# Another order of all operations, and other buffer homes, in a transformer block's forward and backward pass

## The chip, the cores and the metric

One core of a Trainium2 chip runs the whole program in one launch. The metric is the device time of that core in microseconds, the median of the runs of a kernel. TensorE is called PE below, VectorE DVE, ScalarE ACT, GpSimd POOL and SyncE SP.

## The reference

The kernel computes the output of one pre-LN transformer block and all gradients with respect to its inputs, for S = 2048 rows, D = 512, F = 1792, 32 heads of 16, in bf16:

```python
def _A_ref(x, wqkv, wo):                      # attention in a dilated sliding window
    W, dil = 8, 2
    q, k, v = ...                             # (x @ wqkv), 32 heads of 16
    idx = pos[:, None] - (jnp.arange(W) * dil)[None, :]     # rows s, s-2, ..., s-14
    kg, vg = k[:, :, idx], v[:, :, idx]       # gathered: 8 keys and values per row
    attn = softmax(where(idx >= 0, einsum("bhsd,bhswd->bhsw", q, kg) * scale, -1e9))
    o = einsum("bhsw,bhswd->bhsd", attn, vg)
    return o @ wo
def _B_ref(x, w1, b1, w2, b2):
    return gelu(x @ w1 + b1) @ w2 + b2
h  = x + _A_ref(layernorm(x), wqkv, wo)
h2 = h + _B_ref(layernorm(h), w1, b1, w2, b2)
out, vjp = jax.vjp(f, x, wqkv, wo, w1, b1, w2, b2)
return (out, *vjp(grad_out))
```

## The kernel before

The rows are cut into four chunks of 512. For each chunk there are three stages.

- **First stage**: LN1, the q, k, v projections (L616, L270), the dots of queries with eight keys (one DVE product of 128x4096 per two window places, L468, summed by PE with a matrix of ones, L476), softmax, then the weighted values. For these POOL gathers eight shifted copies of v from DRAM (Ro, 2304 KB, L460), DVE multiplies (prbo, L507), PE sums (L516), ACT evicts (ost, L521). Then wo, the residual and LN2, whose output SP transposes on its way (ln2T, L291).
- **Second stage**: the FFN with gelu (weights w, output xb and gl), its output, and its backward pass to the gradient at the attention's output.
- **Third stage**: the attention's gradient. got is the gradient through wo (ACT evicts it from PSUM, L297), prb the products for the gradient of the attention weights (L468). Then the gradients of q, k and v, each from its own gather on POOL (Rq from k_d, Rk from q_d, Rv from go_d), four DVE products per gather (prbq, prbk, prbv, L507), four sums on PE (L516), and four evictions on ACT (gqs, gks, gvs, L521). At the end the gradient through wqkv and the LN1 backward pass (gyr, u, gx, L550 to L559).

The weight gradients need all chunks and so run beside the third stage. Each is a group of 16 matmuls (L270, or L268 where it is issued as four matmuls of 32 columns between two sums) into one PSUM bank, which ACT evicts (L297) into half of a pair buffer: wgs for the FFN (wgs2 and wgs1 where the two are told apart), wgso and wgsq for the attention. A full pair is stored by SP (L287). The last groups read LN1's output back from DRAM (ln1b, L282).

Nothing is scheduled at run time. `Plan.op` records every operation with its engine and the buffers that it reads and writes; `Plan.emit` then emits them in one given order (ORDER) and gives each buffer a given place (HOMES): an SBUF offset in units of 64 bytes or a PSUM bank. So ORDER sets the order of the instructions of every engine, and of the transfers that SP and POOL issue, each in order. HOMES decides which later buffer overwrites which earlier one, and that is a wait as well: an operation that writes into a new buffer must wait until the last reader of the old one at that place is done. The reader may be a store that is still on its way.

```python
        for b, h in zip(self.bufs, homes):
            b.home = h if b.space == "ps" else self.base + h * 64
```

A weight-gradient group ends like this; the pair's store is an operation of its own in ORDER:

```python
        evict(st, lambda: st()[:, n, :], ps, lambda: ps()[:, 0:N], N, key=n, tag="wge" + tag)
        if n:
            PAIR.clear()
            store(None, lambda: dst.rearrange("(a p) d -> p a d", p=P), st, lambda: st(), N / 2, tag="wgst" + tag)
```

Of the kernel before, what the change touches and what calls it, by code (L numbers as in the profile page):

```python
# [159 lines left out]
def kernel(  # L160
# [1026 lines left out]
    10, 12, 0, 14, 69, 1, 16, 17, 11, 21, 13, 23, 9, 8, 50, 29, 30, 51, 52, 27, 53, 54, 26, 46, 31, 55, 19, 249, 28, 42, 47, 2, 354, 3, 48, 49, 43,  # L1187
    37, 4, 174, 5, 355, 60, 44, 61, 56, 57, 45, 62, 172, 59, 67, 6, 63, 7, 173, 64, 66, 18, 65, 171, 80, 175, 68, 176, 276, 81, 82, 177, 274, 181,
    179, 83, 70, 275, 178, 71, 87, 180, 277, 72, 73, 278, 379, 279, 88, 74, 183, 75, 377, 77, 24, 22, 85, 25, 380, 84, 86, 76, 378, 252, 89, 78, 251,
    381, 98, 280, 110, 382, 20, 282, 105, 96, 97, 79, 99, 92, 283, 102, 90, 114, 93, 100, 91, 94, 101, 195, 184, 284, 108, 188, 95, 281, 32, 194, 286,  # L1190
    189, 196, 112, 192, 190, 126, 109, 185, 149, 217, 285, 111, 39, 113, 115, 186, 383, 116, 385, 117, 191, 187, 215, 118, 193, 201, 208, 292, 352,
    211, 291, 146, 289, 119, 293, 120, 213, 288, 386, 384, 202, 387, 297, 121, 389, 203, 122, 128, 298, 182, 58, 287, 127, 299, 598, 305, 353, 132,
    290, 204, 294, 212, 214, 216, 218, 250, 295, 597, 137, 148, 304, 296, 133, 306, 311, 197, 219, 134, 300, 307, 129, 301, 147, 198, 302, 138, 303,
    140, 220, 394, 38, 199, 221, 130, 139, 391, 316, 392, 131, 200, 209, 314, 135, 395, 136, 205, 141, 401, 308, 400, 142, 332, 318, 388, 396, 143,
    393, 315, 150, 402, 320, 317, 144, 319, 152, 151, 156, 153, 154, 159, 480, 321, 158, 322, 155, 157, 161, 398, 323, 324, 325, 160, 162, 163, 326,
    327, 164, 333, 334, 343, 338, 403, 222, 408, 168, 407, 167, 166, 404, 165, 40, 397, 405, 170, 409, 344, 596, 481, 345, 595, 346, 339, 411, 210,
    410, 335, 347, 503, 348, 399, 509, 340, 41, 223, 229, 349, 523, 224, 390, 336, 230, 513, 337, 510, 417, 351, 341, 514, 517, 145, 599, 350, 527,
    518, 423, 505, 528, 504, 535, 507, 536, 421, 524, 519, 342, 515, 506, 419, 533, 508, 520, 418, 534, 360, 516, 231, 529, 243, 358, 511, 525, 356,
    240, 530, 244, 420, 526, 483, 422, 537, 424, 362, 361, 521, 206, 425, 241, 539, 232, 242, 426, 484, 245, 540, 551, 235, 485, 427, 246, 552, 247,
    233, 414, 363, 236, 406, 234, 366, 543, 237, 482, 357, 248, 259, 364, 238, 207, 531, 367, 257, 359, 544, 365, 239, 541, 368, 260, 369, 602, 264,  # L1200
    253, 370, 258, 373, 255, 263, 372, 545, 256, 371, 254, 374, 428, 261, 547, 559, 376, 262, 553, 265, 169, 266, 548, 601, 546, 435, 549, 267, 542,
    270, 429, 271, 608, 560, 568, 610, 561, 849, 563, 562, 861, 15, 554, 855, 564, 269, 841, 550, 856, 859, 569, 842, 565, 268, 839, 490, 566, 862,
    273, 847, 567, 840, 865, 848, 611, 850, 837, 555, 430, 330, 538, 851, 436, 556, 845, 512, 852, 437, 455, 860, 835, 415, 866, 446, 867, 846, 838,
    857, 586, 557, 604, 570, 868, 686, 449, 571, 447, 702, 696, 687, 609, 703, 416, 680, 438, 697, 458, 450, 836, 457, 690, 858, 558, 577, 522, 674,
    605, 532, 441, 439, 619, 448, 681, 676, 451, 575, 442, 440, 572, 606, 677, 412, 573, 675, 672, 691, 574, 700, 443, 456, 587, 600, 454, 607, 765,
    444, 329, 452, 578, 445, 612, 617, 576, 488, 328, 684, 673, 620, 701, 682, 579, 603, 487, 461, 453, 590, 591, 272, 670, 225, 489, 683, 459, 580,
    694, 462, 588, 486, 615, 685, 592, 584, 695, 613, 413, 581, 671, 628, 764, 589, 618, 762, 465, 614, 726, 460, 463, 582, 622, 688, 583, 692, 585,
    633, 693, 593, 624, 616, 431, 678, 623, 626, 594, 631, 466, 679, 625, 706, 930, 753, 627, 707, 927, 629, 891, 763, 714, 468, 106, 659, 464, 469,
    125, 704, 643, 124, 744, 727, 644, 632, 718, 754, 892, 853, 660, 634, 755, 636, 730, 107, 918, 637, 745, 929, 698, 375, 652, 715, 766, 470, 331,
    719, 735, 748, 467, 708, 635, 746, 630, 756, 645, 928, 728, 699, 653, 494, 736, 729, 34, 654, 471, 731, 689, 472, 747, 733, 737, 710, 473, 732,  # L1210
    661, 638, 475, 757, 895, 720, 662, 709, 734, 869, 773, 433, 751, 843, 711, 774, 716, 749, 639, 844, 712, 893, 493, 705, 312, 717, 863, 871, 713,
    875, 721, 309, 750, 795, 655, 752, 646, 777, 477, 723, 796, 872, 476, 760, 791, 739, 722, 474, 758, 313, 784, 432, 738, 740, 479, 780, 778, 879,
    896, 900, 725, 880, 621, 742, 883, 724, 741, 876, 919, 909, 743, 884, 759, 798, 931, 761, 792, 885, 901, 785, 870, 922, 873, 864, 886, 1016, 923,
    103, 874, 881, 781, 35, 789, 1036, 790, 920, 877, 902, 1004, 1037, 910, 1017, 1020, 911, 1010, 1021, 878, 894, 800, 904, 799, 1008, 913, 1006,
    1009, 914, 434, 782, 1011, 897, 663, 1030, 1005, 882, 786, 783, 887, 1031, 801, 889, 921, 1034, 898, 888, 1007, 1014, 787, 491, 656, 310, 899,
    1024, 854, 958, 104, 1025, 492, 1015, 940, 1098, 640, 912, 956, 941, 925, 793, 915, 1035, 1087, 775, 916, 917, 1028, 771, 957, 1029, 776, 903,
    960, 772, 1018, 794, 779, 905, 935, 826, 890, 768, 1096, 1026, 906, 1019, 668, 803, 1069, 936, 495, 827, 937, 1097, 1022, 1070, 1099, 942, 961,
    810, 648, 1060, 965, 943, 924, 804, 657, 926, 828, 1100, 966, 1073, 819, 829, 797, 820, 1012, 831, 788, 1071, 805, 1027, 907, 811, 932, 1061, 226,
    963, 1064, 1078, 1065, 812, 959, 1038, 821, 496, 1062, 1013, 813, 1044, 964, 938, 1079, 814, 647, 1063, 1048, 939, 1066, 949, 1074, 822, 1040,
    770, 908, 945, 1103, 806, 951, 1082, 830, 1032, 950, 1052, 954, 1072, 1053, 1033, 1080, 1049, 946, 1081, 1045, 952, 944, 641, 1023, 1054, 1067,  # L1220
    1102, 1068, 947, 1179, 955, 1120, 664, 1041, 1075, 499, 968, 1088, 1657, 658, 478, 824, 984, 1659, 948, 1042, 1046, 1083, 1658, 1084, 985, 1047,
    1050, 1043, 1085, 1107, 1682, 1051, 1055, 986, 1076, 1077, 953, 991, 987, 1118, 767, 1091, 1121, 992, 1089, 969, 1090, 1111, 769, 1094, 807, 227,
    1116, 1734, 815, 988, 1101, 1119, 1109, 933, 497, 649, 808, 975, 967, 642, 962, 1112, 1129, 1732, 1092, 976, 1086, 802, 970, 1733, 1130, 1093,
    993, 1684, 971, 1110, 1108, 1123, 665, 994, 1057, 1127, 823, 123, 996, 501, 1104, 1180, 1671, 666, 934, 809, 669, 1105, 667, 1226, 1672, 1106,
    1117, 1132, 1227, 1124, 1125, 33, 1058, 977, 1126, 1056, 1822, 1128, 1153, 973, 978, 825, 1134, 979, 1746, 989, 980, 1676, 990, 1137, 498, 816,
    1113, 832, 833, 1114, 650, 1673, 981, 1059, 817, 1144, 1001, 1115, 1677, 1095, 651, 1154, 834, 1170, 1138, 1135, 1133, 1678, 1942, 1039, 1155,
    1709, 1665, 1156, 972, 1158, 1139, 1140, 1142, 818, 1217, 1145, 1679, 1660, 1157, 995, 1680, 1159, 1661, 1666, 1683, 997, 998, 1662, 999, 1663,
    974, 1353, 982, 1667, 983, 1941, 1674, 1000, 1668, 1146, 1122, 1669, 1664, 1675, 1221, 1147, 1681, 1222, 1148, 1670, 1160, 1131, 1161, 1171, 1162,
    1690, 1163, 1172, 1141, 1164, 1136, 1685, 1223, 1686, 1003, 1173, 1691, 1823, 1218, 1181, 1219, 1175, 1220, 1174, 1701, 1687, 1696, 1702, 1703,
    1176, 1692, 1177, 1185, 1707, 1143, 1183, 1224, 1704, 1165, 1182, 1697, 1149, 1344, 500, 1228, 1693, 1184, 1186, 1178, 1698, 1187, 1735, 1736,  # L1230
    1699, 1225, 1700, 1705, 1354, 1166, 1150, 1151, 1737, 1167, 1740, 1168, 1152, 1688, 1469, 1741, 1234, 1689, 1738, 1346, 1739, 1230, 1694, 1742,
    1695, 1743, 1821, 1348, 1744, 1745, 1188, 1345, 1706, 1708, 1349, 1347, 1229, 1350, 1470, 1189, 1351, 1352, 1471, 1232, 1231, 1472, 1473, 1747,
# [88 lines left out]
```

## Time and profile before

| what | before |
|---|---|
| median of 3 runs | 568.17 us (566.8 to 573.35) |
| the profiled run | 562.53 us, span 560.8 us |
| mean granted PE clock | 0.983 |
| PE busy | 535.7 us (96%) |
| DVE busy | 494.5 us (88%) |
| ACT busy | 306.0 us (55%) |
| POOL busy | 24.7 us (4%) |
| HBM read, written | 55.74 MB, 39.40 MB |

Times are read from the profiled run, in us from the start of its span. A row of the timeline or of the groups names the engine, the source line, the operation, and "output<-inputs" by the program's names, with the count behind an x. In brackets stands how long the engine sat idle ahead of it and what ended the wait. The chain of waits runs back from the last instruction: each piece is what the piece behind it waited for. In the rows of stretches stand, behind the length, the busy time and count of PE, PE's weight loads, DVE, ACT and POOL, then the granted clock, the share of the DMA engines and GB/s.

### The profile page before, as it was taken

To read this page: it belongs to the slowest core of one execution; us is meant where nothing else is said; L and a number is where in the kernel's file an instruction comes from. 1 tells how busy PE (TensorE), PEld (TensorE's weight loads), DVE (VectorE), ACT (ScalarE), POOL (GpSimd) and SP (SyncE) were. 2 spreads that over 40 slices of the span, in tenths; PEclk is the share of its full clock that TensorE was granted. 3 is DMA by queue.
4 is the path that set the end of the run, shared out by engine and by line. 5 is a ranking of instruction groups with operands and counts; after the bars stand their busy time and mean duration, and the time that the engine had idled before them with its cause. 6 is when DMAs were issued, how large, how long until landed. Compare 5 with 4: busy or idle time off the path is not lost. (4 is left out here: it accounts for less than half of the span.)

```text
span 560.8 us, 12918 instructions
## 1 busy us (share of the span) xinstructions
PE 535.7 (96%) x5479; PEld 270.5 (48%) x5512; DVE 494.5 (88%) x649; ACT 306.0 (55%) x480; POOL 24.7 (4%) x38
## 2 busy tenths in 40 slices
PE   8999879999999999999999999999986999999996
PEld 4966434444544444444444444465443554555542
DVE  7999999999999998899895096999984999999984
ACT  3975358988999848892441314213112475554332
POOL 1300100020001000000000000000010001000000
PEclk9999979999999999999999999999997999999999
DMA  8999999998998695669999999999995999659456
GB/s 267 241 318 274 333 280 377 201 285 219 278 221 224 190 238 152 166 150 197 261 187 199 229 202 217 293 200 310 220 399 238 315 315 314 290 197 229 105 145 174
DMA packets 218122, 135.32 MB, mean 241 GB/s; under 512 B 168464, under 2 KB 213712, under 8 KB 216016
## 3 DMA queue, kind: packets, MB, share of 16 engines
q1 hardware_dynamic: 214752, 93.07, 73.0%
q0 software_dynamic: 3312, 41.42, 19.1%
q8 instruction: 43, 0.70, 0.5%
q14 instruction: 15, 0.12, 0.1%
HBM read 55.74 MB, written 39.40 MB: 170 GB/s over the span
## 5 line engine op out<-in xcount | busy, mean ns | idle before, releaser
L270 PE MATMUL ps<-goT,w2T 128*128 128x512 bf16 x220 | 53.5, 379 | 0.5 <-DVE r L699 0.4
L297 ACT CAST wgs<-ps 128x512 bf16<-128x512 f32 (+1 forms) x30 | 16.3, 560 | 66.8 <-PE ps L268 29.0
L270 PE MATMUL ps<-w,gl 128*128 128x512 bf16 x215 | 52.1, 379 | 0.5
L270 PE MATMUL ps<-w1T,xb 128*128 128x512 bf16 x219 | 51.7, 379 | 0.3
L468 DVE TENSOR_TENSOR prb<-got,vw 128x4096 bf16<-128x4096 bf16 x16 | 36.0, 2285 | 16.7 <-ACT got L297 16.4
L270 PE MATMUL ps<-ln2T,w 128*128 128x512 bf16 x192 | 46.8, 390 | 0.3 <-DVE xb L848 0.3
L507 DVE TENSOR_TENSOR prbq<-Rq,cfq 128x4096 bf16<-128x4096 bf16 x16 | 36.1, 2278 | 9.0 <-PE ps L516 7.3
L766 ACT ACTIVATE xb<-ps,b1c 128x512 bf16<-128x512 f32 x56 | 35.4, 693 | 12.5 <-DMA g_d<-gl 9.0
L848 DVE SCALAR_TENSOR_TENSOR xb<-xb,ps 128x512 bf16<-128x512 bf16 x56 | 37.2, 681 | 5.5 <-PE ps L270 4.6
L507 DVE TENSOR_TENSOR prbv<-Rv,cfv 128x4096 bf16<-128x4096 bf16 x16 | 36.0, 2284 | 1.6 <-DMA Rv<-go_d 1.5
L507 DVE TENSOR_TENSOR prbk<-Rk,cfk 128x4096 bf16<-128x4096 bf16 x16 | 35.9, 2286 | 1.5 <-PE ps L516 1.2
L507 DVE TENSOR_TENSOR prbo<-Ro,cfo 128x4096 bf16<-128x4096 bf16 x16 | 36.0, 2285 | 1.2 <-PE ps L476 1.1
L468 DVE TENSOR_TENSOR prf<-qt,kt 128x4096 bf16<-128x4096 bf16 x16 | 35.6, 2282 | 0.0
L270 PEld LDWEIGHTS <-xb 128*128 128x128 bf16 x224 | 21.9, 98 | 26.4
L270 PEld LDWEIGHTS <-gl 128*128 128x128 bf16 x224 | 21.5, 98 | 26.9 <-ACT gl L769 1.0
L270 PEld LDWEIGHTS <-w2T 128*128 128x128 bf16 x220 | 21.4, 98 | 26.8 <-issue 1.5
L616 PE MATMUL ps<-ln1T,wqk 128*32 128x512 bf16 x512 | 31.1, 382 | 1.3 <-DVE ln1T L301 1.0
L270 PE MATMUL ps<-gor,gw2in 128*128 128x512 bf16 x129 | 30.6, 379 | 0.3 <-issue 0.2
L270 PEld LDWEIGHTS <-w 128*128 128x128 bf16 x192 | 19.0, 100 | 24.5 <-issue 3.7
L550 ACT ACTIVATE gyr<-ps,rstd 128x512 bf16<-128x512 f32 x16 | 10.9, 682 | 34.2 <-PE ps L270 34.2
L268 PE MATMUL ps<-gw1in,ln 128*32 128x512 bf16 x464 | 28.8, 396 | 0.0
L788 ACT ACTIVATE xb<-xb 128x2048 bf16<-128x2048 bf16 (+1 forms) x16 | 26.9, 1692 | 2.4 <-DVE xb L787 2.4
(194 smaller groups left out, 1028.4 us busy)
## 6 DMA issues: line engine op xcount, KB each, us to landing
Ro<-v_d POOLq DMA_DIRECT2D x4, 2304.0 KB, 11.3
Rq<-k_d POOLq DMA_DIRECT2D x4, 2304.0 KB, 10.9
Rv<-go_d POOLq DMA_DIRECT2D x4, 2304.0 KB, 13.2
Rk<-q_d POOLq DMA_DIRECT2D x4, 2304.0 KB, 15.0
g_d<-gl SPq DMA_DIRECT2D x9, 512.0 KB, 4.5
gh_d<-xb SPq DMA_DIRECT2D x9, 512.0 KB, 3.8
w<-in_B_w_dram SPq DMA_DIRECT2D x2, 1792.0 KB, 8.9
out_dram<-wgs SPq DMA_DIRECT2D x13, 256.0 KB, 3.3
```

Source lines behind the costliest of these rows:

```text
L268: T.matmul(out[32 * a:32 * a + 32, :], lhsT=l[:, 32 * a:32 * a + 32], rhs=r, start=start, stop=stop, skip_group_check=True)
L270: T.matmul(out, lhsT=l, rhs=r, start=start, stop=stop, skip_group_check=True)
L297: fn = lambda: A.copy(out=ap(), in_=pap())
L468: op("DVE", tt_us(4096), lambda g=g, pr=pr: V.tensor_tensor(out=pr(), in0=ql()[:, g, :].unsqueeze(1).to_broadcast([P, W, 512]), in1=_sub(k ...
L507: V.tensor_tensor(out=pr().rearrange("p a j (d h) -> p a j d h", h=H), in0=_sub(R()[:, o0, 0:1], [[st, 2], [512, 4], [32, DH], [1, H]]), i ...
L550: op("ACT", act_us(D, 1, True), lambda: A.activation(out=gyr()[:, j, :], in_=ps(), func=ACT.Copy, scale=rs[:, t:t + 1], accum_out=sg_[:, i ...
L616: T.matmul(ps()[32 * a:32 * a + 32, gg * 512:(gg + 1) * 512], lhsT=_sub(wq_()[:, dc, 0:1], [[DH, H]], sel * D + 4 * g + a), rhs=rhs, start ...
L766: op("ACT", act_us(512, 1), lambda f=f, ps=ps, xb=xb, f0=f0: A.activation(out=xb()[:, f - f0, :], in_=ps(), func=ACT.Identity, bias=b1c[:, ...
L788: op("ACT", act_us(N), lambda xb=xb: A.activation(out=fl(xb), in_=fl(xb), func=ACT.Tanh, scale=GC), w=[xb], tag="tanh", mode=6)
L848: op("DVE", 0.61, lambda f=f, ps=ps, z=z, f0=f0: V.scalar_tensor_tensor(out=z()[:, f - f0, :], in0=z()[:, f - f0, :], scalar=1.0, in1=ps() ...
```

## The change

Only two tables differ, ORDER and HOMES, in nearly all of their numbers. The operations are the same 1948, with the same shapes. The diff, cut to the first line of each table:

```diff
 ORDER = (
-    10, 12, 0, 14, 69, 1, 16, 17, 11, 21, 13, 23, 9, 8, 50, ...
+    10, 24, 0, 25, 1, 8, 12, 11, 23, 14, 15, 69, 17, 29, 19, ...
 )
 HOMES = (
-    2829, 224, 961, 673, 1185, 2549, 2261, 1957, ...
+    1089, 607, 2839, 673, 1185, 2551, 2261, 1473, ...
 )
```

What it does is seen in the engines' rows. Names carry the number of the buffer in this program and two more that tell its place in the order; the numbers differ between the two programs.

POOL's queue in the third stage, before: every row is a gather of 2304 KB or the store of one chunk's gradient (gq, gk, gv).

```order
L460 DMA Rq_1462_41_4915<-k_d_58 128x9216
L460 DMA Rk_1473_40_4969<-q_d_59 128x9216
L287 DMA gq_d_81<-gqs_1396_38_4500 128x2048
L460 DMA Rv_1482_42_5017<-go_d_60 128x9216
L287 DMA gv_d_83<-gvs_1491_43_5088 128x2048
L460 DMA Rq_1546_32_5422<-k_d_58 128x9216
L287 DMA gk_d_82<-gks_1572_34_5617 128x2048
L460 DMA Rk_1596_32_5730<-q_d_59 128x9216
L460 DMA Rq_1638_33_5920<-k_d_58 128x9216
```

The same piece of the queue in the change:

```order
L460 DMA Rq_1458_40_4851<-k_d_58 128x9216
L460 DMA Rk_1460_41_4861<-q_d_59 128x9216
L460 DMA Rv_1496_42_5087<-go_d_60 128x9216
L460 DMA Rq_1525_34_5296<-k_d_58 128x9216
L287 DMA gq_d_81<-gqs_1385_38_4360 128x2048
L287 DMA gv_d_83<-gvs_1452_40_4835 128x2048
L287 DMA gk_d_82<-gks_1552_36_5431 128x2048
L460 DMA Rk_1598_28_5589<-q_d_59 128x9216
L460 DMA Rq_1633_35_5733<-k_d_58 128x9216
```

The three stores, which stood between the gathers, now follow one another behind the fourth gather, and the next Rk stands right behind the gk store.

ACT at the same time, before. The pair wgs1_1496 has the home of the older pair wgs2_1338, which SP stores (second fence); gvs are the evicted gradients of v.

```order
L297 CAST wgs1_1476_41_4980<-ps 128x512
L492 COPY glf_1310_42_4213<-glf_1310_42_4213 32x8x14
L297 CAST wgs1_1463_42_4917<-ps 128x512
L521 ACTIVATE gvs_1491_43_5088<-ps 128x512
L297 CAST wgs1_1496_45_5125<-ps 128x512
L297 CAST wgs1_1476_41_4980<-ps 128x512
L521 ACTIVATE gvs_1491_43_5088<-ps 128x512
L297 CAST wgs1_1496_45_5125<-ps 128x512
```

```order
L282 DMA ro1_1455_41_4895<-o_d1_70 128x2048
L282 DMA ln1b_1456_42_4897<-ln1_d1_62 32x4x512
L287 DMA out_6_dram<-wgs2_1338_39_4316 128x2x512
L287 DMA out_4_dram<-wgs1_1496_45_5125 128x2x512
L287 DMA out_7_dram<-gbs_1382_41_4451 4x128
```

ACT in the change, at the corresponding sinks of the v gradient:

```order
L297 CAST wgs1_1472_39_4908<-ps 128x512
L521 ACTIVATE gvs_1452_40_4835<-ps 128x512
L297 CAST wgs1_1500_43_5123<-ps 128x512
L521 ACTIVATE gvs_1452_40_4835<-ps 128x512
L297 CAST wgs1_1510_39_5225<-ps 128x512
L521 ACTIVATE gqs_1516_38_5263<-ps 128x512
L492 COPY glf_1289_44_4037<-glf_1289_44_4037 32x8x14
```

The number of evictions of each kind is the same. They stand in another succession. Of the pairs here, wgs1_1472 and wgs1_1500 lie where no store reads, and wgs1_1510 over buffers of the attention's gradient.

ACT where the third stage begins, before (got is the gradient through wo, two buffers of two evictions each; gyr and c belong to the FFN's LN backward pass):

```order
L552 ACTIVATE c<-sg 128x1 x2
L297 CAST got_44_3630<-ps 128x1024
L297 CAST got_44_3637<-ps 128x1024
L297 CAST got_44_3630<-ps 128x1024
L297 CAST got_44_3637<-ps 128x1024
L297 CAST wgs_1246_47_3838<-ps 128x512 x2
```

And in the change:

```order
L297 CAST wgs_1164_45_3451<-ps 128x512
L550 ACTIVATE gyr_1141_46_3396,sg<-ps,rstd 128x512
L552 ACTIVATE c<-sg 128x1 x3
L297 CAST got_47_3483<-ps 128x1024
L552 ACTIVATE c<-sg 128x1
L297 CAST got_47_3483<-ps 128x1024
L297 CAST got_51_3517<-ps 128x1024
L297 CAST wgs_1205_51_3545<-ps 128x512 x2
```

Chunk 0's got (got_44_3637 before, got_47_3483 in the change), whose halves stood alternately with those of chunk 1, now stands complete ahead of them.

202 rows, old and new, of tables (HOMES, ORDER) are left out of this document.

## The prediction

> **What bounds the kernel now.** I began with the table of busy time.
>
> ```profile
> PE 535.7 (96%) x5479; PEld 270.5 (48%) x5512; DVE 494.5 (88%) x649; ACT 306.0 (55%) x480; POOL 24.7 (4%) x38
> ```
>
> The matmuls fill 96% of the span, so an order can give back only what PE idles or spends at a lowered clock. The table of stretches says where that is (the first number after the length is PE's busy time, the one behind POOL's is the granted clock):
>
> ```profile
> 60.00:80.00 20.00, 14.12 (x158) 6.67 (x151) 19.69 (x24) 6.87 (x9) 1.04 (x1) 0.86 1.01 311
> 80.00:100.00 20.00, 20.00 (x180) 9.19 (x180) 18.90 (x14) 15.28 (x22) 1.65 (x3) 0.88 1.08 337
> 200.00:220.00 20.00, 19.95 (x94) 9.05 (x93) 19.13 (x37) 10.26 (x15) 0.00 (x0) 1.00 0.75 167
> 300.00:320.00 20.00, 19.89 (x92) 9.07 (x93) 5.16 (x11) 4.56 (x15) 0.00 (x0) 1.00 1.09 213
> 420.00:440.00 20.00, 14.56 (x203) 7.68 (x207) 12.12 (x6) 8.73 (x14) 0.81 (x2) 0.83 0.63 246
> 460.00:480.00 20.00, 18.61 (x286) 9.32 (x281) 18.61 (x12) 12.29 (x25) 1.57 (x3) 1.00 0.96 335
> ```
>
> Through 200 to 320 us PE is full at full clock. Two places stand out. At 60 to 80 us DVE is the full engine (19.69 of 20) and PE waits for it. At 420 to 440 us both are far from full and the clock falls to 0.83. That second hole is followed with the chain of waits and the timeline:
>
> ```profile
> 405.50 19.14 DMA out_dram<-wgs
> 424.75 0.59 ACT wgs L297
> ```
>
> ```profile
> 404.72 0.53 POOL L460 DMA_DIRECT2D Rq<-k_d  x1 [22.56 <-DVE prbv L507]
> 405.50 27.89 SPq L287 DMA_DIRECT2D out_dram<-wgs  x2
> 406.54 0.53 POOL L460 DMA_DIRECT2D Rk<-q_d  x1 [1.29 <-PE ps L268]
> 407.06 0.54 POOL L287 DMA_DIRECT2D gq_d<-gqs  x1
> 409.13 0.53 POOL L460 DMA_DIRECT2D Rv<-go_d  x1 [1.53 <-PE ps L516]
> ...
> 415.12 3.63 PE L268 MATMUL ps<-gw1in,ln 128*32 128x512 bf16 x64
> 416.90 2.29 DVE L507 TENSOR_TENSOR prbq<-Rq,cfq 128x4096 bf16<-128x4096 bf16 x1 [0.24 <-DMA Rq<-k_d]
> ...
> 424.75 1.07 ACT L297 CAST wgs<-ps 128x512 bf16<-128x512 f32 x2 [11.77 <-DMA out_dram<-wgs]
> 425.38 1.05 PE L516 MATMUL ps<-prbv,S 128*32 128x512 bf16 x8 [6.64 <-ACT wgs L297]
> ...
> 426.19 5.29 PE L268 MATMUL ps<-gw1in,ln 128*32 128x512 bf16 x64
> 426.48 2.29 DVE L507 TENSOR_TENSOR prbq<-Rq,cfq 128x4096 bf16<-128x4096 bf16 x1 [7.28 <-PE ps L516]
> ```
>
> Read it backwards. DVE waits 7.28 us for a PSUM sum, PE waits 6.64 us for ACT to free a bank, and ACT waits 11.77 us to write a weight-gradient pair (wgs) whose SBUF home still holds an older pair that is being stored. That store was issued at 405.50 among three gathers of 2304 KB and a 512 KB store, all issued within 4.4 us, and it landed 19.14 us later. The tile's own row says how unusual that is:
>
> ```profile
> DMA to landing us min/median/max: 2.1/3.3/19.1
> ```
>
> **The sum goes against the profiled run**, 562.53 us with a span of 560.8; the median of the three timed runs is 568.17, 1.0% more, so I scale at the end.
>
> *Term 1, the stall.* The idle is 6.64 us. Then 64 sums of L268 take 5.29 us where the same 64 took 3.63 us at 415 us, and eight of L516 take 1.05; the same eight take 0.61 elsewhere (a row below). That is 1.66 + 0.44 = 2.1 us of lowered clock. Together **8.7 us**, on the path, since DVE and ACT stood still with PE. In the changed order the large transfers are further apart: Rq and Rk stand side by side in POOL's queue as before, but the gradient store gq is moved behind two further gathers, Rv and the next Rq. With other homes, the pairs that ACT evicts in this stretch go over pairs that SP stored well before these gathers, or over buffers that no store reads; none goes over a store that is queued beside them, as here. I count the whole 8.7 as gone. If the new home's store is late as well, it is a rival, below.
>
> *What is late next there.* The products. The first prbq began 12.18 us after its gather's issue and was held by the gather for 0.24 us, so with the stall gone DVE meets the gathers:
>
> ```profile
> Rq<-k_d POOLq DMA_DIRECT2D x4, 2304.0 KB, 10.9
> Rv<-go_d POOLq DMA_DIRECT2D x4, 2304.0 KB, 13.2
> Rk<-q_d POOLq DMA_DIRECT2D x4, 2304.0 KB, 15.0
> ...
> gq_d<-gqs POOLq DMA_DIRECT2D x1, 512.0 KB, 17.4
> gk_d<-gks POOLq DMA_DIRECT2D x1, 512.0 KB, 6.6
> ```
>
> From here on DVE is nearly as full as PE (18.61 against 18.61 at 460 to 480), so a late gather passes through to PE. If the moved Rq lands like the median Rk, the product waits 15.0 - 11.9 = 3.1 us more; if as now, 0. I take **+1.5**, the middle, since the pair is issued as closely as before but with one transfer fewer beside it.
>
> *Term 2, the first stage.* Three sums stand in a row ahead of the first FFN matmul, each waiting for a product of its own:
>
> ```profile
> 75.47 0.61 PE L516 MATMUL ps<-prbo,S 128*32 128x512 bf16 x8 [0.88 <-ACT tmv L297]
> 77.02 0.61 PE L516 MATMUL ps<-prbo,S 128*32 128x512 bf16 x8 [0.94 <-DVE prbo L507]
> 79.22 1.04 PE L516 MATMUL ps<-prbo,S 128*32 128x512 bf16 x8 [1.59 <-DVE prbo L507]
> 80.20 3.59 PE L270 MATMUL ps<-ln2T,w 128*128 128x512 bf16 x8
> ```
>
> In the change two sums, a transposition of the attention output and two FFN steps stand ahead of the third sum. The FFN step needs the transposed LN2 output:
>
> ```profile
> 73.31 3.16 SPq L291 DMA_TRANSPOSE ln2T<-ln  x1
> ```
>
> ```profile
> ln2T<-ln SPq DMA_TRANSPOSE x4, 5.2
> ```
>
> It lands at about 73.3 + 5.2 = 78.5 us, so PE cannot start the FFN more than 80.20 - 78.5 = 1.7 us sooner. DVE's products, 2.29 us each, are as many and stand in the same order, and DVE stays the full engine, so most of that is only idle moved. Bounds 0 and 1.7; I take **-0.7**, nearer 0. The lowered clock behind it (eight FFN matmuls 3.59 us; at 200 to 220 us 94 take 19.95, or 1.70 for eight) I leave as it is: 1.9 us more if it goes.
>
> [...] By the row it can win up to the 1.9 us; I keep them for the low end of the range.
>
> *Term 3, the wait for ln1b.*
>
> ```profile
> PE ps L270 <- DMA ln1b<-ln_d: 1.1, 1, 1.1
> ```
>
> It sits behind a load that took 12.77 us beside two gathers. The change issues these loads earlier on SP, between the pairs' stores, in another succession. Between -1.1 and, if a load meets a gather as closely as now, +1.5 (the longest ln1b landing, 12.7, less its median, 11.2): I take **-0.5**.
>
> *At nothing:* the attention gradient's first eviction.
>
> ```profile
> 320.08 4.00 ACT L297 CAST got<-ps 128x1024 bf16<-128x1024 f32 x4 [3.98 <-DMA out_dram<-wgs]
> ```
>
> ```profile
> DVE prb L468 <- ACT got L297: 16.4, 1, 16.4
> ```
>
> Chunk 0's pair of these moves ahead of chunk 1's, between earlier operations of ACT. That may start DVE's products some 8 us earlier (half of the 16.4). PE is busy 19.89 of 20 us there: the weight gradients cover it. Without that cover it would be worth the 8 us; with it DVE gets a reserve that the rest of the kernel can use only where DVE is the later engine. The start, the second stage and the tail (the last eviction at 555.8 us and a store) hold the same operations in slightly different succession: 0, by 1 us either way, since PE's idle there is a few tenths.
>
> Sum: -8.7 + 1.5 - 0.7 - 0.5 = **-8.4 us**, 554.1 for the profiled run; times 568.17 / 562.53 that is -8.5, and **559.7 us** as a median.
>
> **The rivals.**
>
> *The stall only moves.* The new order has its own reuse of a home behind a store. The closest I find is at the gradient stores: gq, gv and gk now stand in one piece on POOL, and the next sink of the value gradients takes a home that the gk store must leave first; ACT's queue behind it holds the gradient transposes' copies, the LN1-backward evictions and a weight-gradient eviction, and PE waits for those banks. For it: gq_d took 17.4 us beside gathers, against it: gk_d took 6.6. With 6.6 nothing is late; with 17.4 the sink is held about 17.4 - 6.6 = 10.8 us, of which, as at 424.75 (11.77 held, 6.64 passed on), about 6.1 reach PE, plus 2.1 of lowered clock: +8.2, which leaves about **568**. [...]
>
> *Half of it comes back as late gathers.* Each of three chunks brings three gathers. If in each one gather lands as the slow third (15.0 instead of 10.9 to 13.2, say 2 us later) and DVE has no reserve, three times 2 is 6 in place of my 1.5: -3.9, about **564**.
>
> *Slower: Rk held behind the three stores.* POOL works in order. Rk of the third chunk stands right behind the gk store, which can't be issued before the last of its four sinks is evicted:
>
> ```profile
> 452.36 0.54 POOL L287 DMA_DIRECT2D gk_d<-gks  x1 [12.10 <-ACT gks L521]
> 452.89 0.53 POOL L460 DMA_DIRECT2D Rk<-q_d  x1
> ```
>
> That is so today too, with the first prbk at 466.84, 14.0 us later. In the change POOL has no gather between these stores that could go ahead. If the sinks come late, Rk lands late, and DVE and PE both stand. From a delay of some 10 us (it must use up the -8.4) it decides; at 14 us, the gather's own 15.0 us served wholly after the products have run out, and with two half-clock stretches of 2.1 us it is -8.4 + 14 + 4.2 = +9.8, about **578**. Against it: the sinks follow PE's sums, which come earlier once the stall has gone.
>
> *It does not do anything that counts.* With PE full at 96% in both, and DVE as full as PE at 460 to 480 us, the 8.7 us could be given back to DVE's own waits: terms 2 and 3 alone, -1.2, are left, about 567. The trace speaks against it, since DVE itself lost 7.28 us in that stall and would be ahead by as much.
>
> **How the numbers follow.** My forecast, by its own terms from -11 to -5: 0.58, about 557 to 563. Late gathers at 564: 0.15. Stall moved or no effect, 567 to 568: 0.15. Slower, about 571 to 578: 0.12. For 8 in 10 I leave out a tenth at each end: the range is 554 (all early terms at their good bound, -8.7 - 1.7 - 1.9 - 1.1 = -13.4) to 571. 1% is 5.7 us, which is also about what a measurement of this kernel can tell from no change: faster below 562.5, same to 573.9. Of my own case 0.53 lies below 562.5, of the late gathers' 0.06; so faster 0.59, slower by over 1% 0.10, same the rest.
>
> **What would show it.** Right: no ACT wait of over 3 us for a wgs store in the chain after 400 us, the clock at 1.00 at 420 to 440 us, PE over 19 there, and DVE's idle before the L507 products put down to gathers. The got wait is about 8 us instead of 16.4. Wrong: a wait of ACT for gk_d or wgs in 430 to 465 us with the clock at half after it (stall moved), rows of L507 with DMA Rq, Rk or Rv of over 4 us in sum (late gathers), or a POOL row of Rk that waits for gks and a DVE idle behind it (the slower case). The 60 to 80 us stretch should stay at about 14 to 15 us of PE.

## The result: 0.988 of the time before, and the stall gone

| | before | changed |
|---|---|---|
| median of 20 runs each | 567.22 us (557.43 to 593.59) | 555.64 us (552.36 to 575.75) |
| ratio of the runs | | 0.9876, 95% interval 0.9846 to 0.9907 |
| a second time, beside b_h2 below | 566.66 us (11 runs) | 553.87 us (6 runs), ratio 0.9811, 0.9761 to 0.9861 |
| the profiled run | 562.53 us, span 560.8 | 555.56 us, span 553.8 |
| mean granted PE clock | 0.983 | 0.995 |

Single runs of one kernel scatter here by some per cent; the ratios leave out the disturbed runs, and where a profile below is of a long run, only the named place is read from it.

The page's first part, after:

```profile
PE 534.0 (96%) x5440; PEld 263.1 (48%) x5440; DVE 495.1 (89%) x649; ACT 307.2 (55%) x480; POOL 24.2 (4%) x38
```

The busy times hardly differ, so the 7.0 us of span were idle time and clock. The table of stretches of the changed kernel, for the same stretches as before:

```profile
60.00:80.00 20.00, 14.74 (x233) 8.53 (x231) 18.78 (x24) 10.58 (x13) 1.03 (x1) 1.00 0.96 315
80.00:100.00 20.00, 19.72 (x172) 8.89 (x176) 19.40 (x14) 13.98 (x20) 1.66 (x3) 0.91 0.89 311
...
300.00:320.00 20.00, 20.00 (x94) 9.11 (x93) 13.92 (x28) 6.78 (x17) 0.00 (x0) 1.00 0.96 181
...
400.00:420.00 20.00, 20.00 (x324) 10.14 (x320) 15.82 (x14) 6.79 (x14) 1.58 (x3) 1.00 1.06 367
420.00:440.00 20.00, 18.87 (x298) 9.42 (x288) 19.22 (x12) 8.10 (x16) 1.58 (x3) 1.00 0.93 356
...
460.00:480.00 20.00, 20.00 (x348) 10.41 (x344) 19.65 (x10) 11.78 (x22) 1.06 (x2) 1.00 1.00 398
```

At 420 to 440 us PE's busy time went from 14.56 to 18.87 us and the clock from 0.83 to 1.00; at 460 to 480 us, where PE had waited for ln1b, from 18.61 to 20.00. At 60 to 80 us PE's busy time is little changed (14.12 and 14.74 us), while the clock reads 1.00 in place of 0.86; term 2 below comes back to that. The timeline of the place where the stall was:

```profile
404.46 0.53 SPq L287 DMA_DIRECT2D out_dram<-wgs  x1
404.71 0.53 POOL L460 DMA_DIRECT2D Rq<-k_d  x1 [25.95 <-DVE prbv L507]
407.15 0.53 POOL L460 DMA_DIRECT2D Rk<-q_d  x1 [1.91 <-PE ps L516]
415.50 1.14 DVE L486 STREAM_TRANSPOSE cfq<-glf 128x512 bf16<-128x512 bf16 x1 [3.22 <-DMA out_dram<-wgs]
416.00 0.53 POOL L460 DMA_DIRECT2D Rv<-go_d  x1 [8.33 <-PE ps L516]
417.88 4.45 DVE L507 TENSOR_TENSOR prbq<-Rq,cfq 128x4096 bf16<-128x4096 bf16 x2
428.56 0.54 POOL L287 DMA_DIRECT2D gq_d<-gqs  x1
436.93 0.61 PE L516 MATMUL ps<-prbk,S 128*32 128x512 bf16 x8 [1.13 <-DVE prbk L507]
```

A store of a pair stands beside the gathers here too, and it is late again: DVE waits for it until 415.50, 11.0 us after its issue. But the buffer that takes its home is a coefficient buffer (cfq) on DVE, needed when PE has work of its own, and PE is busy 20.00 us of 20. The late transfer is still there; what has gone is the path from it to PE. (My description of the change spoke of the homes of pairs alone and so missed this one.) In the second profile of the changed kernel, with a span of 552.1 us, the same store was issued at 401.85, 2.2 us ahead of Rq, and landed after 4.0 us; nothing waited for it there, and the 1.13 us wait of PE for prbk is gone too.

### The profile page after: what moved, and what is told of

It reads as the page before. It is cut to its first block, busy times and chain, and to the rows that moved or that the text cites. A ratio compares the mean times of both kernels' runs of the same rounds, so it can differ in the third digit from the quotient of the medians.

```text
span 553.8 us, 12777 instructions
## 1 busy us (share of the span) xinstructions
PE 534.0 (96%) x5440; PEld 263.1 (48%) x5440; DVE 495.1 (89%) x649; ACT 307.2 (55%) x480; POOL 24.2 (4%) x38
## 3 DMA queue, kind: packets, MB, share of 16 engines
q0 software_dynamic: 3312, 41.42, 19.1%
## 5 line engine op out<-in xcount | busy, mean ns | idle before, releaser
L270 PE MATMUL ps<-w,gl 128*128 128x512 bf16 x212 | 48.1, 379 | 0.0
L468 DVE TENSOR_TENSOR prb<-got,vw 128x4096 bf16<-128x4096 bf16 x16 | 36.3, 2282 | 12.2 <-PE ps L270 7.1
L270 PE MATMUL ps<-ln2T,w 128*128 128x512 bf16 x188 | 45.3, 389 | 0.3
L784 ACT ACTIVATE x<-xb 128x2048 bf16<-128x2048 bf16 (+1 forms) x16 | 27.0, 1697 | 3.5 <-DMA out_dram<-h2s 2.1
L270 PE MATMUL ps<-gor,gw2in 128*128 128x512 bf16 x120 | 28.5, 379 | 0.0
## 6 DMA issues: line engine op xcount, KB each, us to landing
Ro<-v_d POOLq DMA_DIRECT2D x4, 2304.0 KB, 12.2
Rq<-k_d POOLq DMA_DIRECT2D x4, 2304.0 KB, 11.4
```

Source lines behind the costliest of these rows:

```text
L270: T.matmul(out, lhsT=l, rhs=r, start=start, stop=stop, skip_group_check=True)
L468: op("DVE", tt_us(4096), lambda g=g, pr=pr: V.tensor_tensor(out=pr(), in0=ql()[:, g, :].unsqueeze(1).to_broadcast([P, W, 512]), in1=_sub(k ...
L784: op("ACT", act_us(N), lambda xb=xb, x2=x2: A.activation(out=fl(x2), in_=fl(xb), func=ACT.Square), r=[xb], w=[x2], tag="x2")
```

## The experiments

**b_home: the one reuse.** Two homes are exchanged, and nothing else:

```diff
 HOMES, in units of 64 bytes:
-    wgs1_1496: 224 (the pair wgs2_1338 before it),  wgs1_1524: 2967
+    wgs1_1496: 2967,  wgs1_1524: 224
```

> The kernel before, with the homes of two weight-gradient pairs exchanged so that the eviction which waited 11.8 us goes over a buffer that was last read long before; order as before. Theory 'reuse' (the gain is that one home behind a late store): the ACT wait of 11.8 us and PE's 6.6 us are gone, the clock at 420 to 440 us is 1.00, the store itself still lands some 19 us after its issue, and the profiled span is 552 to 553 us instead of 560.8, as low as the changed kernel's 553.8 or lower. Rival 'order' (the many other moves bring the gain, and late gathers take the stall's place in the old order): half or more of the 8.7 us comes back as waits for Rk or Rv, the span 556 to 558.

Measured: ratio 0.9932 (0.987 to 0.9994), the profiled run 551.74 us with a span of 550.0. Its stretches:

```profile
400.00:420.00 20.00, 20.00 (x328) 9.88 (x330) 18.05 (x15) 5.64 (x12) 2.12 (x4) 1.00 0.99 351
420.00:440.00 20.00, 20.00 (x348) 10.83 (x340) 19.96 (x10) 9.10 (x14) 1.07 (x2) 1.00 1.00 371
```

The row of the tile wgs, and ACT's eviction in the timeline beside the late store, which was issued at 403.41:

```profile
DMA to landing us min/median/max: 2.8/4.2/18.9
```

```profile
412.56 0.59 ACT L297 CAST wgs<-ps 128x512 bf16<-128x512 f32 x1 [0.64 <-PE ps L268]
```

The store lands as late as ever, 18.9 us, and nobody waits: ACT evicts at 412.56 where it had evicted at 424.75. PE is full at 400 to 440 us. In this run two numbers give 10.8 us of span, more than the whole change. About 1 us of that is chance: the first product prb starts at 320.99 us here and at 322.04 before, ahead of the exchange, where the two kernels do not differ. The rival, that late gathers would take the stall's place, falls for this run. But it is the fastest of 12: four lay at 552 to 558, five at 562 to 565 and three above, and their median, 563.81 us, is level with the 564.58 us of the kernel before beside them. What those above 562 us waited for has no profile here.

**b_store and b_ahead: the store issued sooner.** The same store, moved in SP's queue by some 28 us (b_store; to 377.83 us), or by 1.6 us, to just ahead of the reloads of ro (b_ahead):

```diff
 ORDER, SP's queue:
-    ..., gbs, ro, ro, ln1b, store of wgs2_1338, ...
+    store of wgs2_1338, ... gbs, ro, ro, ln1b, ...       (b_store)
+    ..., gbs, store of wgs2_1338, ro, ro, ln1b, ...      (b_ahead)
```

> The kernel before, with one operation moved: the store of the pair that was overwritten is issued about 35 us earlier, ahead of the three gathers; homes as before. Theory 'reuse': the store lands within 3 to 5 us of its issue, the eviction finds its home free, span 552 to 553 us. Rival 'order': 556 to 558 us, as above. If the earlier store holds up the weight gradients' transposed loads behind it on SP, PE waits there and the gain is smaller by that wait.

> The kernel before with the late store moved ahead of the two reloads ro and the load of ln1b on SP, by some 1.6 us, so that it is issued shortly ahead of the gather Rq as in the changed kernel; homes and gathers as before. If the place in SP's queue and against the gather makes it late, it lands after 4 to 11 us instead of 19.1, ACT waits under 4 us, PE under 1 us, and the span is 551 to 555, unless the reloads behind it are late in its place (PE then waits for ro at about 411 us, 560 to 563). If it is the company of the gathers as such, it lands after 17 to 20 us and the span stays at 560 to 562.

Measured: b_store 554.34 us at best and 565.31 us as the median of 6 (564.58 for the kernel before beside it); b_ahead 556.73 us at best of 4, three of them above 565. Neither has a ratio. The row of the tile wgs in b_store, from a run of 565.2 us:

```profile
DMA to landing us min/median/max: 2.1/3.4/4.6
```

The store, out of the gathers' way, lands after at most 4.6 us, and ACT waits for it no more. But now the reload of ro, issued at 405.29 where the store had been issued at 405.50, takes 14.7 us and holds PE for 7.5, as PE's longest wait and the chain of waits show:

```profile
PE ps L268 <- DMA ro<-o_d: 7.5, 1, 7.5
```

```profile
405.29 14.69 DMA ro<-o_d
420.02 9.54 PE ps L268 x128
```

In b_ahead's profiled run (span 578.6 us) the same two views show PE behind ro again:

```profile
PE ps L268 <- DMA ro<-o_d: 13.9, 1, 13.9
```

```profile
417.08 20.16 DMA ro<-o_d
```

The store, which was to be issued shortly ahead of Rq, came 1.0 us behind it in this run and landed after 16.0 us:

```profile
415.61 0.53 POOL L460 DMA_DIRECT2D Rq<-k_d  x1 [31.64 <-DVE prbv L507]
416.66 0.38 SPq L287 DMA_DIRECT2D out_dram<-wgs  x1
```

So b_ahead did not test what it was made for, and the lateness isn't the store's own. Nor does the store hand it on: in the profile of b_first (below), where store and homes are those of before, the store took 23.7 us and ro 17.1, and PE waited 7.1 us for ro. What goes with it is seen under a_wgo.

**b_rv and b_rk: which gather?** One gather is taken from beside the store:

```diff
 ORDER, POOL's queue (before: Rq, Rk, gq, Rv, gv):
+    Rq, Rk, gq, gv, Rv     (b_rv)
+    Rq, gq, Rv, Rk, gv     (b_rk)
```

> The kernel before, with one gather moved: Rv of chunk 2 is issued on POOL behind the gv store instead of ahead of it, so that only two gathers and the gq store are in flight beside the late store; homes and all other orders as before, so the reuse stays. Theory 'company' (the store is late because of the bytes in flight beside it, 7.7 MB before, 5.4 MB now): it lands after 12 to 14 us instead of 19.1, ACT waits 4 to 6 us instead of 11.8, PE under 1 us, clock 1.00, span 552 to 555 us. Rival (the store is held by something else on SP's queue): it lands after some 19 us as before, and the span stays at 560 to 561.

> The kernel before with the gather Rk issued behind Rv on POOL instead of ahead of it: beside the late store there is one gather (Rq) in the first 3.6 us, not two, and the same three in the end. If a store waits for the gathers that are issued within a microsecond or two of it, it lands with Rq's end, after 11 to 13 us instead of 19.1, ACT waits 3 to 5 us, PE under 1 us, and the span is 552 to 555. If it waits for all bytes in flight or for SP's own queue, it lands after 18 to 20 us and the span stays at 560 to 562.

Measured: b_rv 1.0055 (1.0011 to 1.0099), b_rk 0.9995 (0.9937 to 1.0053). ACT's wait and the row of the tile wgs in b_rv:

```profile
ACT wgs L297 <- DMA out_dram<-wgs: 11.9, 1, 11.9
```

```profile
DMA to landing us min/median/max: 2.1/4.0/18.6
```

And in b_rk, from a run of 586.5 us:

```profile
ACT wgs L297 <- DMA out_dram<-wgs: 11.0, 1, 11.0
```

```profile
DMA to landing us min/median/max: 2.1/3.2/19.2
```

With Rv 28 us away, or Rk 5 us away, the store lands as late. My theory that the spread of the gathers shortens the landing falls. The gq store beside it was not taken away. What goes with 11 us in the changed kernel and 19 before is seen under a_wgo.

**b_hw: is it the reload of ro?** As b_home, and the first step of wo's gradient (the wait that b_store showed), goes back in the order:

```diff
 ORDER, PE's part (step 1855 is the first of the gradient of wo):
-    ..., wg1, 1855, wg1, ..., sums, wg1, ..., transpositions of gq, ...
+    ..., wg1, wg1, ..., sums, wg1, ..., transpositions of gq, 1855, ...
```

> The kernel before with the exchanged homes of b_home, and one more move: the first step of the gradient of wo, which reads the reloaded attention output ro some 8 us after that load is issued, goes behind the sums and the transposition that followed it (about 20 us later). Theory 'slack' (what SP issues beside the gathers lands after 8 to 20 us, differently from run to run; a kernel is fast if nothing there is needed sooner): no run has a wait for ro or for the wgs store, the timed runs gather at 551 to 556 us, where those of b_home lay at 552 to 558 and at 562 to 565. Rival 'other' (the spread of b_home's runs has another source): the runs still fall into the same two groups.

Measured: ratio 0.9886 (0.9818 to 0.9954), 6 runs from 551.4 to 563.68, still scattered. Its profiled run (560.83 us) shows one reason. PE's longest wait, ACT's behind it, and the row of the tile wgs:

```profile
PE ps L532 <- ACT wgs L297: 3.8, 1, 3.8
```

```profile
ACT wgs L297 <- DMA out_dram<-wgs: 6.9, 1, 6.9
```

```profile
DMA to landing us min/median/max: 2.1/3.3/25.3
```

The late store took 25.3 us in this run, and the second pair, which the exchange had put into its home, waited for it. In this run ro landed late as well, after up to 17.8 us, and PE did not wait for it. So the need for ro alone does not explain the scatter: in b_home and here I had only moved the reuse some 10 us back, and that is not always enough. That b_home's runs above 562 us had the same wait is likely, not shown.

**b_h2 and b_h3: no reuse of a stored home.** Both pairs in homes whose last reader is no store; b_h2 with the step of b_hw as well, b_h3 without it:

```diff
 HOMES:
-    wgs1_1496: 224,  wgs1_1524: 2967
+    wgs1_1496: 2967,  wgs1_1524: 2229
```

> The kernel before with the first step of the gradient of wo behind the sums as in b_hw, and the two pairs in homes that no store reads at all: in b_hw the second pair had been given the home of the late store, and where that landed after 25.3 us ACT waited again by 6.9 us and PE by 3.8. Theory 'reuse' (only a home behind the late store stops PE): no ACT wait for a wgs store after 400 us, the profiled span 549 to 552 us, the timed runs mostly at 551 to 555, below the changed kernel's. Rival 'whatever lands late' (loads that are needed at once stop PE as often): the runs still reach 558 to 564 in half of the cases, with waits for ro, gw1in or ln1b in the profile.

> The kernel before with two numbers changed: the two pairs in the homes of b_h2 that no store reads, and the order of the kernel before, the first step of the gradient of wo included. Theory 'reuse': as b_h2, 0.976 to 0.986 of the kernel before, timed runs mostly at 551 to 556, no ACT wait for a wgs store after 400 us in the profile. Rival 'ro' (the move of that step is needed as well, since the reload of ro lands late in some runs): 0.986 to 0.995, with a wait of PE for ro of 2 us or more at about 411 us in some profile.

Measured: b_h2 0.9806 (0.9748 to 0.9865), its 7 runs at 551.55 to 555.03 but for two (562.01 and 571.1); b_h3 0.9885 (0.9798 to 0.9973), its 6 runs at 553 to 554, once 560.13, twice 566.33. Beside b_h2 on the same chip:

> The changed kernel as it is, on the same chip as b_h2, to be compared with it: 554 to 556 us as in its first runs, 0.985 to 0.991 of the kernel before. If b_h2's theory holds it is the slower of the two by 1 to 4 us.

Measured 0.9811 (0.9761 to 0.9861). So the kernel before with two homes and one step moved is as fast as the changed one, within the measurement, and b_h3, with two numbers alone, has the ratio that the changed kernel had at first (0.9876). That the step of b_hw is needed is not shown: the intervals of b_h2 and b_h3 overlap, and no wait for ro stands in b_h3's profile. The profiled runs are of 562.01 and 566.33 us. The row of wgs and PE's longest wait, first of b_h2, then of b_h3:

```profile
DMA to landing us min/median/max: 2.6/3.4/17.4
PE ps L268 <- DMA gw1in<-gh_d: 5.1, 1, 5.1
```

```profile
DMA to landing us min/median/max: 2.8/4.5/25.4
PE ps L268 <- DMA gw1in<-gh_d: 9.6, 1, 9.6
```

The store is late in both, up to 25.4 us, and after 400 us no eviction of ACT waits for a store: the cure holds. But other transfers of SP still stop PE in these two runs, the transposed load gw1in, and ln1b by 1.6 and 2.7 us. My rival, that whatever lands late stops PE, holds to that extent; why gw1in was late was not followed.

**a_wgo: take the slack back.** In the changed kernel the first three steps of wo's gradient go ahead by about 12 us:

```diff
 ORDER, PE's part:
-    ..., wg1, ..., sums of gq, 1861, 1862, transposition, sum, 1863, ...
+    ..., 1861, wg1, ..., 1862, wg1, ..., 1863, wg1, ..., sums of gq, transposition, sum, ...
```

> The changed kernel with one thing taken back: the first three steps of the gradient of wo are moved ahead by about 12 us, so that PE needs the last reloaded ro some 10 us after its load is issued, and not 21. Theory 'slack': PE waits for ro by 5 to 11 us, the clock falls to half behind it, the span rises from 553.8 by 6 to 12 us, most of what the change brought. Rival 'reuse alone' (only the overwritten pair mattered): no wait over 1 us, span 553 to 555.

Measured: 0.99 (0.9849 to 0.995), span 555.1. No wait for ro. The row of ro, first of the changed kernel, then of a_wgo:

```profile
DMA to landing us min/median/max: 3.9/11.2/22.3
```

```profile
DMA to landing us min/median/max: 4.0/4.5/5.2
```

With the same four loads in the same order on SP the longest took 22.3 us in one run and 5.2 in the other. So this run could not tell: the need was there 10 us after the issue, the lateness wasn't. I keep the theory of slack as argued for ro, and as shown for the pair's home only.

The lateness does not come at random, though. The last two loads of ro in the changed kernel, where Rq was issued at 404.71, then both in a_wgo:

```profile
405.08 0.94 SPq L282 DMA_DIRECT2D ro<-o_d  x2
```

```profile
402.63 0.89 SPq L282 DMA_DIRECT2D ro<-o_d  x2
404.92 0.53 POOL L460 DMA_DIRECT2D Rq<-k_d  x1 [25.95 <-DMA ro<-o_d]
```

SP and POOL each issue in their own order, and which is ahead at this place differs from run to run: the changed kernel's second profile, with 4.0/4.7/5.2 in the same row of ro, has these two loads ahead of Rq as a_wgo has. The landings follow that:

| trace | transfer of SP | issued, against Rq | landed after |
|---|---|---|---|
| before | store of the pair | 0.8 us behind | 19.1 us |
| changed | store of the pair | 0.25 us ahead | 10.9 us |
| changed | last two ro | 0.4 and 0.8 us behind | 17.0 and 22.3 us |
| changed, second profile | store of the pair | 2.2 us ahead | 4.0 us |
| changed, second profile | last two ro | 1.6 and 1.1 us ahead | 4.4 and 5.2 us |
| b_store | last two ro | 1.5 and 2.0 us behind | 14.7 and 17.4 us |
| b_hw | store of the pair | 3.7 us behind | 25.3 us |

Over all 14 traces, of the stores of wgs and the loads ro and ln1b that SP issued within 4 us of this Rq, the 25 that came half a microsecond or more ahead of it landed after 3.6 to 6.1 us, the 26 that came over 0.1 us behind it after 12.2 to 25.4; the 10 between took 4.7 to 17.4. This is read off afterwards: no experiment moved Rq alone.

**a_both: what the changed kernel still waits for.** The eviction of another pair, which waits 5.1 us for a store at 363 us, gets another home, and the cfq above goes behind the four products:

```diff
 HOMES:  -wgs2_1341: 288    +wgs2_1341: 1925
 ORDER, DVE's part:  -cfq, cfk, prbq x4    +cfk, prbq x4, cfq
```

> The changed kernel with two spots mended: the one eviction that still waits 5.1 us for a store gets another home, and the coefficient transposition on DVE that waits 3.2 us for the store among the gathers is moved behind the four products that follow it. Theory 'DVE's lag passes on' (from 420 us on what DVE loses, PE waits for later): PE's waits of 0.6 us for the eviction and 1.1 us for the product prbk go, span 551.5 to 552.5 instead of 553.8. Rival: both waits were covered, span 553.5 to 554.

Measured: 0.9899 (0.9828 to 0.997), span 555.9: nothing gained. A wait of DVE and one of PE:

```profile
DVE prbq L507 <- DMA Rq<-k_d: 3.9, 1, 3.9
```

```profile
PE ps L516 <- DVE prbk L507: 1.7, 2, 1.1
```

DVE now waits 3.9 us for the gather Rq in place of 3.2 for the store, and PE's wait of 1.1 us for prbk stays. That fits the rival, but decides little: the store was issued 1.0 us ahead of Rq in this run and landed after 5.7 us, so there was no late store to be freed from, and the changed kernel's second profile, without either wait, has the shorter span of 552.1.

**b_first: the first stage alone.**

```diff
 ORDER, PE's part:
-    sum, sum, sum, ff1, ff1, transposition
+    sum, sum, ff1, ff1, sum, transposition
```

> The kernel before with the first stage's term alone: the third of the three sums that wait for DVE's products goes behind the first two FFN steps, as in the changed kernel; all else as before. By the prediction's term 2: 0 to 1.7 us less, 0.7 expected, and no more since ln2T lands at 78.5 us; the FFN's first matmul starts at 79 to 80 us and the stretch of 60 to 80 us keeps PE at 14 to 15. Rival: the sums were the wait, and the whole 2.5 us and the lowered clock's 1.9 go, 4 us less by 105 us. The stall at 418 us stays in either case.

Measured: 1.0029 (0.998 to 1.0078). In the timeline the FFN now starts ahead of the third sum, and waits for the transposed LN2 output:

```profile
77.16 1.04 PE L516 MATMUL ps<-prbo,S 128*32 128x512 bf16 x8 [1.26 <-DVE prbo L507]
79.29 3.60 PE L268 MATMUL ps<-ln2T,w 128*32 128x512 bf16 x32 [1.09 <-DMA ln2T<-ln]
82.66 1.01 PE L516 MATMUL ps<-prbo,S 128*32 128x512 bf16 x8
```

It starts 0.9 us sooner than at 80.20, but the third sum comes at 82.66 in place of 79.22, and its consumers with it. The ratio, good to some 3 us, cannot tell 0.7 us from nothing; the trace shows no gain: the first matmul on the second stage's gl starts at 102.6 us, against 101.2 to 102.3 in the nine traces with the old first stage.

## Why the prediction was right, point by point

The forecast was -8.4 us of the profiled run and 559.7 us in the median; the spans gave -7.0 and, the second time, 552.1 against 560.8, -8.7; the ratios are 0.988 and 0.981 where 559.7 / 568.17 is 0.985. The median over all runs came out 4 us under the forecast. The two spans of the one changed kernel differ by 1.7 us, so terms of that size can't be told apart here.

- **Term 1, the stall (-8.7): right in mechanism and size.** The 6.64 us of PE went, and so did the lowered clock (0.50 at 425.3 to 427.0 us before, against 1.00 over 420 to 440 us now). b_home's profile shows that freeing the one reused home ends that stall, and b_h3's ratio (0.9885 against 0.9876) that two homes can account for the whole gain. One step of it failed: I argued that the large transfers stand further apart and that no home beside them is reused. In the first profile the store lands late all the same, and a home is reused; it is the engine behind the home that differs. In the second the store, issued 2.2 us ahead of Rq, landed after 4.0 us; that a greater distance of the gathers makes a store early was not shown (18.6 us in b_rv, 19.2 in b_rk).
- **What is late next (+1.5): the size came right by luck, the cause was wrong.** I expected prbq to wait for its gather. In the changed kernel it did not; PE waited 1.13 us for a product prbk at 436.93, behind a DVE that had lost 3.22 us to the late store. In the second profile that wait is absent, and prbq waits 0.5 us for its gather.
- **Term 2 (-0.7): nothing that shows.** The first FFN matmul came at 80.63 us, not sooner:

```profile
76.77 0.61 PE L516 MATMUL ps<-prbo,S 128*32 128x512 bf16 x8 [1.62 <-DVE prbo L507]
78.96 0.61 PE L516 MATMUL ps<-prbo,S 128*32 128x512 bf16 x8 [1.58 <-DVE prbo L507]
...
80.63 3.45 PE L270 MATMUL ps<-ln2T,w 128*128 128x512 bf16 x8
```

The bound of 1.7 us by ln2T was sound, and b_first ran into it. Two waits of 1.6 us took the place of 0.88, 0.94 and 1.59. On the clock, this pair of traces cuts both ways: with these two waits the clock was granted in full at 60 to 80 us and fell to 0.91 at 80 to 100, where before it had been 0.86 and 0.88. No run shows what lowers it there. The eight matmuls behind still took 3.45 us. The share of the clock that is missing over these 40 us comes to 5.2 us before and 1.8 in the changed kernel, so part of the 1.9 us that I kept for the low end did come; but it is 3.4 us in each of seven other traces with the old first stage, and 1.6 to 3.6 in the four with the new one. The order can't be credited with it from one pair of traces.
- **Term 3, ln1b (-0.5): -1.1.** No wait of PE for ln1b is left in the changed kernel.
- **At nothing, the attention gradient's start: right.** The first product starts at 310.64 us, not at 322.04 (11.4 us sooner, where I had said 8), DVE's busy time at 300 to 320 rose from 5.16 to 13.92, and PE was full in both.
- **Not foreseen: about +1.7**, the rest of -8.7 + 1.1 - 1.1 against -7.0. Of it 0.6 us is traced, PE behind an eviction that waited 5.14 us for a store until 368 us, a small repeat of the old stall; the others are tenths that I could not name. The whole 1.7 is what the changed kernel's two profiles differ by, and neither this eviction's wait nor that for prbk is in the second.
- **The rivals.** "The stall only moves" happened on DVE and at 368 us, at about a fifth of its price (1.13 and 0.6 us of PE against 8.2) in one profile and not at all in the other. The queue behind the gk store did no harm: nothing waited for Rk. The same kind of transfer runs through all of it: a 256 KB store took 3.3 us in the median of the kernel before, and 19.1 where SP issued it 0.8 us behind Rq on POOL.

## What to carry to other kernels

A buffer's home is a dependency that the program's text does not show: when one wait lasts far over the median of its transfer (here a landing of 19.1 us against 3.3), look which older buffer lies there and who still reads it, and move that home before the order. At this place transfers of 128 to 512 KB issued behind a gather of 2304 KB landed after up to 25.4 us, those issued half a microsecond or more ahead of it after 6.1 at most; so the ones behind should have nobody who needs them, or their space, within some 25 us. Taking one gather away from beside the store did not make it early (18.6 us in b_rv, 19.2 in b_rk). The issues of SP and POOL changed places here from run to run (the last load of ro 0.8 us behind Rq in one profile of the changed kernel, 1.1 ahead in the other), so look at more than one profile before you call a landing a property of the kernel. A table of thousands of numbers may owe its gain to two of them, and exchanging just those tells.

## What was not expected of the hardware

Transfers of 128 to 512 KB that SP issued behind the start of a gather of 2304 KB took 12.2 to 25.4 us at this place, where the median store of a pair takes 3.3 in the kernel before; those issued half a microsecond or more ahead of it took 3.6 to 6.1. The same loads in the same order of the same kernel took up to 22.3 us in one run and 5.2 in another, as their place against the gather changed by 2 us. The landing of the store did not depend on a second or third gather being near: 19.1, 18.6 and 19.2 us with Rk and Rv beside it, with Rv away and with Rk later. Why being behind costs so much is open.
